# Causal attention with a second, transposed score product in place of probability transposes

## The chip, the cores and the metric

The kernel runs on one core of one Trainium2 chip. Its engines are PE (TensorE, matrix products), DVE (VectorE), ACT (ScalarE), POOL (GpSimd) and SP (SyncE, which here issues DMAs). Times are device microseconds of one execution; the metric is the median over the runs. Each kernel also has one profiled execution, whose instructions and transfers are what the views of the trace show.

## The reference

One layer on 2048 tokens of 1024 features, all in fp32: a layer norm, an attention block with a memory ("infini-attention", 32 heads of 32 features, 4 segments of 512 tokens), a residual, a second layer norm, a mixer block (its own norm, 1024 to 3584 to 1024 with a GELU) and a residual. The attention of a segment s:

```
logits = einsum("bhqd,bhkd->bhqk", qs, ks) * scale + mask      # causal
a_dot  = einsum("bhqk,bhkd->bhqd", softmax(logits), vs)
num    = einsum("bhld,bhde->bhle", phi(qs), M)
den    = einsum("bhld,bhd->bhl", phi(qs), z)[..., None] + 1e-6
o      = g * num / den + (1 - g) * a_dot                       # g = sigmoid(beta) of the head
M      = M + einsum("bhld,bhle->bhde", phi(ks), vs)
z      = z + einsum("bhld->bhd", phi(ks))
```

M (32x32 per head) and z (32 per head) begin at zero, so segment 0 reads nothing from the memory, and what segment 3 would add is never read.

## The kernel before, in words

Products run on PE in a rounded fp32 type. To keep fp32's accuracy each factor is split into a high part (rounded) and a low part (what is left), and a product is three matmuls: high x high, high x low, low x high. A split is a copy on ACT (or DVE) for the high part and a subtraction on DVE (or POOL) for the low one.

The program goes through two halves of 1024 tokens, two segments each. In a half, `attention` loops over 8 groups `g` of four heads and over the half's two segments `sl`. Each such pair is a unit `u`. `dense` computes a unit's projections of keys, queries and values: 3 x 8 x 3 = 72 matmuls of 512 columns, in transposed form (feature by token). Beside them run, by `interleave`, the four heads of the unit before, step by step (`heads`, `slot`). While one unit's projections run, the score products and the softmax of the unit before are done.

Each head is a *slot* of six steps (`PLAN`), and the slots are pipelined over three heads: `cur` has its scores computed, `p1` its probabilities transposed, `p2` multiplied with v. In a slot:

- `qk` (L515): the scores of 128 queries by 128, 256, 384 or 512 keys, as one matmul whose 96 contraction rows hold the three partial products (`stack`, L363, lays them out by DMA from kh, kl, qh, ql). DVE then reduces with the mask (L524): it writes minus the scaled scores to `pr` and their minimum to `mx`; ACT takes the exponential with the row's extreme as bias and sums the row (`soft`, L532).
- `norm` (L534): a reciprocal of the row sums (128x2) on DVE and, on POOL, the multiplication of the probabilities by it and by 1 - g.
- `ptr` (L542): ten 128x128 transposes of the probabilities on PE per head, into PSUM. ACT copies them out as the high part `pth` (L557), `sub` (L560) makes the low part `ptl` on DVE from PSUM and `pth`.
- `av` (L564): eight matmuls into `po`, whose weights are 64 columns wide (v's high and low parts side by side). `av_out` (L582) adds the two halves of `po`, and for the group's last head adds the memory's part on POOL and stores the group.

`late` (L457) handles what is left of a unit beside the next one's projections: transposes of v (L460), the memory read (`pm`, products with queries as weights, so that the result is token by feature; a small reciprocal, L472; a product with it, L474; four transposes back, `pom`, L504) and the memory update (`pmm`, L489, L490). These small matmuls are put one by one between the transposes and PV matmuls (`one_small`).

The order of the instructions on the engines in this stage is that in which the program emits them, subject to the scheduler. After attention, `wo_first` runs the first output products beside the last unit's heads. PSUM has two banks for scores (`qk`), two for transposes (`pt`), one for PV (`av`) and three for projections and small products (`d`).

## Time and profile before

| | us |
|---|---|
| median of 3 runs (2358.27 to 2362.35) | 2360.43 |
| span of the profiled execution | 2354.0 |
| PE busy in that span | 2288.6 |
| DVE busy | 1575.9 |
| ACT busy | 1228.8 |
| POOL busy | 1058.4 |

The profiled execution's span runs from its first to its last instruction and is 6.4 us under the median of the runs. In the page's rows a group of instructions is named by its line, engine and operation, then `out<-in` by the program's names, shapes and count; behind the first bar its busy time in us and the mean duration in ns, behind the second the time for which the engine idled just before these instructions and what ended most of it. In a timeline a row is start (us), duration (us), engine, line, operation, names, shapes and count; an idle time before it stands in brackets with what ended it. Matmul durations include the pipeline's fill, so that consecutive matmuls overlap in these rows.

The attention stage takes about 42 to 520 us and 939 to 1440 us of the span; the rest is the mixer, which the change does not touch.

### The profile page before, as it was taken

To read this page: it belongs to the slowest core of one execution; us is meant where nothing else is said; L and a number is where in the kernel's file an instruction comes from. 1 tells how busy PE (TensorE), PEld (TensorE's weight loads), DVE (VectorE), ACT (ScalarE), POOL (GpSimd) and SP (SyncE) were. 2 spreads that over 40 slices of the span, in tenths; PEclk is the share of its full clock that TensorE was granted. 3 is DMA by queue.
4 is the path that set the end of the run, shared out by engine and by line. 5 is a ranking of instruction groups with operands and counts; after the bars stand their busy time and mean duration, and the time that the engine had idled before them with its cause. 6 is when DMAs were issued, how large, how long until landed. Compare 5 with 4: busy or idle time off the path is not lost.

```text
span 2354.0 us, 35355 instructions
## 1 busy us (share of the span) xinstructions
PE 2288.6 (97%) x11769; PEld 1893.4 (80%) x11769; DVE 1575.9 (67%) x3334; ACT 1228.8 (52%) x2557; POOL 1058.4 (45%) x1037
## 2 busy tenths in 40 slices
PE   7999999999999999999999999999999999999999
PEld 6888888878878887888888877778887888888887
DVE  6777777776655565777777777564566676566753
ACT  5676776785453444777777776363343233222321
POOL 4444444445243442555555545252444564255430
PEclk9999999999999999999999999999999999999999
DMA  5333333345365654433333334466557976576762
GB/s 172 95 89 91 86 81 87 83 115 174 127 196 171 192 161 137 124 83 84 88 83 85 89 93 132 152 198 175 168 176 251 341 254 204 160 251 222 255 219 94
DMA packets 322719, 355.36 MB, mean 151 GB/s; under 512 B 26190, under 2 KB 218730, under 8 KB 322538
## 3 DMA queue, kind: packets, MB, share of 16 engines
q1 hardware_dynamic: 259370, 316.40, 44.7%
q10 hardware_dynamic: 63168, 36.71, 5.2%
q8 instruction: 93, 1.52, 0.3%
q14 instruction: 88, 0.72, 0.1%
HBM read 226.59 MB, written 76.09 MB: 129 GB/s over the span
## 4 chain that ended last, share of the span: by engine, by line
PE 73%; DVE 9%; ACT 7%; DMA 4%; POOL 3%; issue 3%; SPq 1%; ACTq 0%; POOLq 0%; DVEq 0%
PE po L1235 21%; PE bps L856 8%; PE dps L856 5%; PE ppt L555 5%; PE po L575 4%; PE cps L856 4%; PE pqk L523 3%; PE kps L114 2%; PE kps L115 2%; PE kps L116 2%; PE vps L114 2%; PE vps L115 2%; PE vps L116 2%; PE qps L114 2%; PE qps L115 2%
## 5 line engine op out<-in xcount | busy, mean ns | idle before, releaser
L539 POOL TENSOR_SCALAR pr<-pr,nm,gate 128x128 f32<-128x128 f32 (+3 forms) x512 | 320.9, 636 | 400.6 <-DVE nm L536 293.1
L532 ACT ACTIVATE pr<-pr,mx 128x256 f32<-128x256 f32 (+3 forms) x512 | 287.6, 562 | 179.1 <-DVE mx L524 176.5
L524 DVE CUSTOM_DVE_ANT_0 pr<-pqk,mask 128x256 f32<-128x256 f32 (+3 forms) x512 | 243.5, 484 | 37.7 <-PE pqk L523 35.2
L562 DVE TENSOR_TENSOR ptl<-ppt,pth 128x512 fp32r<-128x512 f32 (+1 forms) x384 | 227.2, 597 | 59.5 <-ACT pth L557 57.4
L555 PE MATMUL ppt<-ident,pr 128*128 128x128 f32 x1280 | 223.2, 277 | 1.8 <-DVE ptl L562 1.8
L557 ACT CAST pth<-ppt 128x512 fp32r<-128x512 f32 (+1 forms) x384 | 194.0, 518 | 42.3 <-PE ppt L555 36.7
L1245 DVE TENSOR_TENSOR c<-c,po 128x512 f32<-128x512 f32 x160 | 105.3, 683 | 146.1 <-PE po L1235 146.1
L555 PEld LDWEIGHTS ppt<-ident,pr 128*128 128x128 f32 x1280 | 164.4, 140 | 32.1 <-DVE ptl L562 3.6
L91 POOL TENSOR_TENSOR wl<-wr,wh 128x1024 fp32r<-128x1024 f32 x53 | 126.8, 2392 | 90.8 <-DVE wh L88 31.0
L523 PE MATMUL pqk<-ks,qs 96*128 96x256 f32 (+3 forms) x512 | 163.3, 320 | 1.6 <-DVE mx L524 1.6
L575 PE MATMUL po<-ptl,vs 128*64 128x512 f32 (+3 forms) x512 | 154.8, 312 | 5.9 <-DVE ptl L562 5.7
L575 PE MATMUL po<-pth,vs 128*64 128x512 f32 (+3 forms) x512 | 156.3, 327 | 2.2 <-ACT pth L557 2.1
L1235 PE MATMUL po<-w2h,zh 128*128 128x512 f32 x378 | 120.8, 389 | 0.0
L523 PEld LDWEIGHTS pqk<-ks,qs 96*128 96x128 f32 x512 | 96.6, 189 | 27.1 <-DVE mx L524 7.0
L536 DVE RECIPROCAL nm<-mx 128x2 f32<-128x2 f32 x256 | 42.2, 165 | 109.0 <-ACT pr L532 108.7
L968 POOL TENSOR_TENSOR s<-r 128x512 f32<-128x512 f32 x28 | 43.1, 1540 | 158.9 <-DVE sa L984 117.6
L1105 POOL TENSOR_TENSOR w2r<-w2r 128x512 f32<-128x512 f32 x54 | 85.4, 1593 | 62.3 <-DMA w2r<-in_B_w 62.3
L856 PE MATMUL bps<-zh,sa 128*128 128x512 f32 x336 | 110.7, 390 | 1.6 <-DVE u L998 1.6
L856 PE MATMUL bps<-zh,sb 128*128 128x512 f32 x336 | 111.0, 391 | 0.9 <-DVE u L1010 0.9
L114 PE MATMUL kps<-yh,wh 128*128 128x512 f32 (+1 forms) x264 | 110.2, 417 | 0.6 <-ACT yh L144 0.6
L114 PE MATMUL vps<-yh,wh 128*128 128x512 f32 x256 | 109.0, 426 | 0.2 <-ACT omt L505 0.2
L114 PE MATMUL qps<-yh,wh 128*128 128x512 f32 x256 | 106.8, 417 | 0.0
(237 smaller groups left out, 6748.0 us busy)
## 6 DMA issues: line engine op xcount, KB each, us to landing
hr<-h_dram SPq DMA_DIRECT2D x112, 448.0 KB, 4.8
w2r<-in_B_w SPq DMA_DIRECT2D x122, 256.0 KB, 4.4
r<-in_B_w SPq DMA_DIRECT2D x56, 512.0 KB, 4.6
h_dram<-ht ACTq DMA_DIRECT2D x84, 256.0 KB, 3.8
ks<-kh SPq DMA_DIRECT2D x256, 64.0 KB, 2.0
qs<-qh SPq DMA_DIRECT2D x256, 64.0 KB, 2.0
wr<-in_A_wo SPq DMA_DIRECT2D x32, 512.0 KB, 4.0
wx<-in_B_w SPq DMA_DIRECT2D x56, 256.0 KB, 3.7
```

Of the source, the lines that this page charges most:

```text
L114: nc.tensor.matmul(ps, ah, bh, start=first, stop=False)
L115: nc.tensor.matmul(ps, ah, bl, start=False, stop=False)
L523: nc.tensor.matmul(pqk[:, :n], u["qs"][j][:, i * P:(i + 1) * P], u["ks"][j][:, 0:n], start=True, stop=True)
L524: nc.vector.tensor_tensor_reduce(out=st["pr"][:, offs[i]:offs[i] + n], in0=pqk[:, :n], in1=mask[:, 512 - n:512], op0=ALU.add, op1=ALU.min, ...
L532: nc.scalar.activation(pi, pi, AF.Exp, bias=mx[:, i:i + 1], scale=-1.0, accum_out=mx[:, 4 + i:5 + i])
L539: nc.gpsimd.tensor_scalar(pi, pi, nm[:, 4 + k:5 + k], gate[:, 1, 4 * g + j:4 * g + j + 1], op0=ALU.mult, op1=ALU.mult)
L555: nc.tensor.transpose(ppt[:, o:o + P], pr[:, offs[i] + jk * P:offs[i] + (jk + 1) * P], ident)
L557: nc.scalar.copy(pth[:, base:base + w], ppt[:, :w])
L562: nc.vector.tensor_tensor(o, x0, x1, op=ALU.subtract)
L575: nc.tensor.matmul(po[:, P * jk:], v, st[part][:, koff[jk]:koff[jk] + w], start=(jk, part) == (0, "pth"), stop=(jk, part) == (2, "ptl"))
L856: nc.tensor.matmul(ps, x_[:, c, :], y_[:, c, :], start=first and c == 0 and n == 0, stop=last and c == 3 and n == 2, skip_group_check=True)
L1235: nc.tensor.matmul(ps, x_[:, k], y_[k], start=opens and k == 0 and i == 0, stop=closes and k == self.KP - 1 and i == 2, skip_group_check=True)
```

## The change

Per head, in place of transposed probabilities:

1. The scores are computed as before and reduced with the mask, now only for the row's maximum (`peak`; the reduce writes its elementwise result back into the PSUM tile).
2. The four columns of row extremes (128x4) are transposed on PE (`turn`), copied out in a high part on ACT and a low part on DVE (`row_high`, `row_low`), and sent by two DMAs into rows 96 and 97 of the head's stacked queries `qs`. The stacked keys `ks` have ones in these two rows.
3. The scores are computed a second time, with keys as weights, in transposed form (key by query), over 98 contraction rows: the two added rows subtract the maximum (`scores`).
4. ACT takes the exponential from PSUM into SBUF (`soft`, three per head), POOL zeroes what lies above the diagonal (`cut`), ACT copies the high part (`upper`) and DVE subtracts for the low one (`lower`), both now from the SBUF tile.
5. v's tile is 96 wide: high, low and 32 columns of ones. `po` has 96 rows, of which the last 32 hold the row sums. ACT copies rows 32 to 95 in two instructions (`av_low`). Once per four heads DVE takes the reciprocal of the sums (128x512) and multiplies by it and by 1 - g (`av_out`).

The memory read is turned: the memory is expanded to block-diagonal weights (`blocks`, `mzf`), and numerator and denominator come out feature by token, in 2 x 3 matmuls of 512 columns. ACT adds epsilon, DVE takes a 128x512 reciprocal and multiplies. The memory update becomes 8 matmuls instead of 12, with z kept as one column.

The order of the work is written out: `PLAN` is one list of operations per slot, in which D is one of the 18 projection matmuls that a slot runs beside, m one small matmul of the line, and a digit the head's place in the pipeline (0 cur, 1 the one before, 2 two before). `AT` gives the matmul positions at which the copies, splits and loads of a unit are emitted, `AFTER` those of the small work. PE, DVE, ACT and POOL are held to the order of emission (`in_order(*ATT)`).

```diff
-RA, RH, RS, PD, PS = 1.3, 14, 0.7, 20, 3
-PLAN = ('q1 S2', 'q0 n0 a0', 'q2 t0 a1', 'q3 n2 s0 o', 't1', 's1 t2')
+RA, RH, RS, PD, PS = 1.3, 42, 0.7, 20, 3
+PLAN = ('0q2 0q1 m 2v D D 0x2 m 1t0 1e0 D 1k0 0x1 2o m 1t1 1t3 D 0q3 D 1e1 1t2 1c0 0q0 D D 1k1 1e2 0x3 0x0 '
+        '1s0 D D 0g 1ah0 1k2 D 0h 0l D m 1c1 1al0 1c2 D D D 1s1 m 1s2 D D m m 1ah2 D 1ah3 1ah1 1al1 1al3 '
+        '1al2 D').split()
+AFTER = dict(pkh=3, pkl=3, vh=0, vl=1, den=0, rec=0, mem=0, upd=7)
...
+        def peak(st, i):
+            n = P * (i + 1)
             nc.vector.tensor_tensor_reduce(
-                out=st["pr"][:, offs[i]:offs[i] + n], in0=pqk[:, :n], in1=mask[:, 512 - n:512],
-                op0=ALU.add, op1=ALU.min, scale=-SCALE, scalar=3.0e38, accum_out=st["mx"][:, i:i + 1])
-            soft(st, i)
...
+                out=st["pqk", i][:, :n], in0=st["pqk", i][:, :n], in1=mask[:, 512 - n:512],
+                op0=ALU.add, op1=ALU.min, scale=-1.0, scalar=3.0e38, accum_out=st["mx"][:, i:i + 1])
+        def turn(st):
+            st["pmx"] = psum.tile([P, 512], F32, tag="qk", name="pmx", bufs=2)[0:4, 0:P]
+            nc.tensor.transpose(st["pmx"], st["mx"][:, 0:4], ident)
+        def row_high(st):
+            st["mr"] = ab.tile([4, 2, P], F32R, name="mr", bufs=2)
+            nc.scalar.copy(st["mr"][:, 0, :], st["pmx"])
+        def row_low(st):
+            mr, qs = st["mr"], st["u"]["qs"][st["j"]]
+            nc.vector.tensor_tensor(mr[:, 1, :], st["pmx"], raw(mr[:, 0, :]), op=ALU.subtract)
+            for k in range(2):
+                nc.sync.dma_start(raw(qs[96 + k:97 + k, :]).rearrange("o (i q) -> o i q", i=4), raw(mr[:, k, :]))
+        def scores(st, jk):
...
+            nc.tensor.matmul(st["pst", n][:, o:o + 512 - P * jk], u["ks"][j][:, jk * P:(jk + 1) * P],
+                             u["qs"][j][:, jk * P:512], start=True, stop=True)
+        def soft(st, n):
+            st["p", n] = ab.tile([P, 512], F32, name="pf", bufs=NF)[:, 0:WIDTH[n]]
+            nc.scalar.activation(st["p", n], st["pst", n][:, 0:WIDTH[n]], AF.Exp, scale=SCALE)
+        def upper(st, n):
+            st["h", n] = ab.tile([P, WIDTH[n]], F32R, name=f"pth{n}", bufs=1 + (n == 1))
+            nc.scalar.copy(st["h", n], st["p", n])
+        def lower(st, n):
+            st["l", n] = ab.tile([P, WIDTH[n]], F32R, name=f"ptl{n}", bufs=1 + (n == 1))
+            nc.vector.tensor_tensor(st["l", n], st["p", n], raw(st["h", n]), op=ALU.subtract)
...
+            nc.scalar.copy(u["ot"][b, :], po[32:64, :])
+            nc.scalar.copy(u["den"][b, :], po[64:96, :])
         def av_out(st):
             nc.vector.tensor_tensor(ot[b, :], po[0:32, :], ot[b, :], op=ALU.add)
             if j == 3:
-                if u["omt"] is not None:
+                nc.vector.reciprocal(den, den)
+                nc.vector.scalar_tensor_tensor(ot, ot, gcol[:, 1, g:g + 1], den, op0=ALU.mult, op1=ALU.mult)
+                if u["s"] > 0:
                     nc.gpsimd.tensor_tensor(ot, ot, u["omt"], op=ALU.add)
...
+                def shifted(ps):
+                    read["d"] = tmp("rd")
+                    nc.scalar.activation(read["d"], ps, AF.Identity, bias=eps)
+                def bottom(ps):
+                    then(AFTER["den"], lambda: shifted(ps))
+                    then(AFTER["rec"], lambda: nc.vector.reciprocal(read["d"], read["d"]))
+                def divided(ps):
+                    u["omt"] = ab.tile([P, 512], F32, name="omt", bufs=1)
+                    nc.vector.scalar_tensor_tensor(u["omt"], ps, gcol[:, 0, g:g + 1], read["d"], op0=ALU.mult, op1=ALU.mult)
+                for n, last in ((1, bottom), (0, top_)):
+                    products(("num", "dn")[n], [(lambda ps: ps, x_[:, n], y_)
+                                                for x_, y_ in ((mzh, pqh), (mzh, pql), (mzl, pqh))], last)
```

More of the change, by code (lines that the diff above doesn't have):

```diff
@@ L378, in smalls @@
[L378 to L391 removed]
+                u[name][j] = st
@@ new lines, in dense @@
+            if s > 0:
+                pq = phi(qps, None, position("qe"), position("qr"), position("pq"))
+            at(position("ql"), lambda: low("ql", qps, "qh"))
+            for j in range(4):
+                at(position(f"q{j}"), partial(stacked, "qs", "qh", "ql", (0, 0, 1), (j,)))
+            yield
+            vps = yield from product("v")
+            vt = tmp("vt")
+            at(position("vt"), lambda: nc.scalar.copy(vt, vps))
+            vs = VS[u["n"] % 2]
+            u["omt"] = None
@@ L1279, in pre @@
                     yield
-        interleave(wo_first(half, hts, pre()), rest, RA, RH, RS)
+        with in_order(*END):
+            interleave(wo_first(half, hts, pre()), rest, RA, RH, RS)
+        acts.pop("last")
         if half == 0:
```

503 lines of the change are left out of this document (257 added, 246 removed).

## The prediction

> **What bounds the kernel now.** I read the page first (span, chain), then the busy times of two stretches of the attention stage, then the instructions of TensorE (PE) and VectorE (DVE) in order of time. A *unit* is what the attention loop does for one group of four heads and one segment of 512 tokens: 72 projection products, and beside them the four heads of the unit before. There are 32 units, 16 in each half of the kernel.
>
> ```profile
> span 2354.0 us, 35355 instructions
> PE 73%; DVE 9%; ACT 7%; DMA 4%; POOL 3%; issue 3%; SPq 1%; ACTq 0%; POOLq 0%; DVEq 0%
> ```
> ```profile
> 104.60:168.40 63.80, 62.08 (x379) 52.06 (x378) 48.00 (x147) 44.72 (x115) 30.01 (x38) 1.00 0.33 83
> 1188.70:1251.60 62.90, 62.16 (x378) 52.04 (x377) 48.73 (x149) 45.29 (x116) 33.15 (x41) 1.00 0.33 84
> ```
> ```profile
> 104.62 0.48 PE L114 MATMUL kps<-yh,wh 128*128 128x512 f32 x1
> ...
> 168.41 0.48 PE L114 MATMUL kps<-yh,wh 128*128 128x512 f32 x1
> ...
> 1188.71 0.48 PE L114 MATMUL kps<-yh,wh 128*128 128x512 f32 x1
> ...
> 1251.65 0.48 PE L114 MATMUL kps<-yh,wh 128*128 128x512 f32 x1
> ```
> The columns of the stretches are length, then busy time of PE, weight loads, DVE, ACT and POOL, granted clock, DMA share and GB/s. The four rows after them are the first key product of a unit, so two units (a *pair*) take 63.79 us in the first half and 62.94 us in the second. PE is busy for 62.1 of them at clock 1.00, DVE for 48 to 49 (77%), ACT for 45, POOL for 30 to 33. The attention stage is bound by what PE is given; DVE has some 7 us of slack per unit.
>
> **PE's part of the change.** What a product costs in the stream is the distance from its start to the next start, not its own duration.
>
> ```profile
> 1207.17 0.22 PE L523 MATMUL pqk<-ks,qs 96*128 96x128 f32 x1
> 1207.23 0.39 PE L575 MATMUL po<-pth,vs 128*64 128x512 f32 x1
> 1207.46 0.39 PE L575 MATMUL po<-ptl,vs 128*64 128x512 f32 x1
> 1207.69 0.34 PE L575 MATMUL po<-pth,vs 128*64 128x384 f32 x1
> 1207.87 0.34 PE L575 MATMUL po<-ptl,vs 128*64 128x384 f32 x1
> ...
> 1209.47 0.28 PE L575 MATMUL po<-pth,vs 128*64 128x256 f32 x1
> 1209.59 0.28 PE L575 MATMUL po<-ptl,vs 128*64 128x256 f32 x1
> ...
> 1211.33 0.60 PE L555 MATMUL ppt<-ident,pr 128*128 128x128 f32 x4
> 1211.69 0.48 PE L114 MATMUL vps<-yh,wh 128*128 128x512 f32 x1
> 1212.01 0.40 PE L115 MATMUL vps<-yl,wh 128*128 128x512 f32 x1
> ```
> ```profile
> 1231.71 0.28 PE L555 MATMUL ppt<-ident,pr 128*128 128x128 f32 x1
> 1231.74 0.31 PE L386 MATMUL pm<-mzh,pql 128*128 128x132 f32 x1
> 1231.89 0.51 PE L555 MATMUL ppt<-ident,pr 128*128 128x128 f32 x3
> ```
> So 512 columns cost 0.23 us, 384 cost 0.175, 256 cost 0.12, 128 cost 0.06. Four transposes cost 0.36, and the product behind them 0.32 instead of 0.23. A lone transpose with a narrow product behind it costs 0.18, 0.06 of it the product's; I take 0.14 for a lone one.
>
> The change removes 40 probability transposes per unit (with what they cost the product behind each run) and the memory read's 12 products and 4 transposes. It adds, per head, four score products (96 rows plus the two rows of the maximum) and one transpose of the maxima. The widening of PV from 64 to 96 output rows changes no column count, so I cost it at nothing. New streams per unit:
> - projections 72 x 0.23 = 16.6; scores twice, 2 x 4 x (0.23 + 0.175 + 0.12 + 0.06) = 4.7; PV with its two parts also 4.7: 25.9 us;
> - transposes of maxima and of v, 8 x 0.14 = 1.1: 27.0;
> - segments 0, 1, 2: four key transposes 0.56 and the memory update 4 x 0.12 + 4 x 0.06 = 0.72; segments 1, 2, 3: the memory read 6 x 0.23 = 1.38.
>
> That is 28.3, 29.7, 29.7 and 28.4 us for segments 0 to 3: 58.0 and 58.1 us per pair against 63.8 and 62.9. With 8 pairs in each half: 8 x (5.8 + 4.8) = **85 us less, if PE never waits** (the last unit of a half runs beside the output products, also at PE's rate; I count it alike). About 1 us of waits per pair that the old rows show (62.1 busy of 62.9 to 63.8) I leave in: 16 us given back.
>
> **DVE's part.** The subtractions and the reduce with the mask stay in number. Small reciprocals go; in their place come two reciprocals over a whole 128x512 tile: the row sums out of PV, once per unit, and the memory's denominator in segments 1 to 3. No row shows one that wide; the nearest:
>
> ```profile
> L536 DVE RECIPROCAL nm<-mx 128x2 f32<-128x2 f32 x256 | 42.2, 165 | 109.0 <-ACT pr L532 108.7
> L472 DVE RECIPROCAL rg<-rg 128x8 f32<-128x8 f32 x48 | 9.6, 200 | 1.0
> L70 DVE RECIPROCAL gate<-bb 128x32 f32<-128x32 f32 x1 | 0.3, 299 | 0.0
> L586 DVE TENSOR_TENSOR ot<-po,ot 32x512 f32<-32x512 f32 x128 | 87.0, 680 | 6.6 <-ACT ot L580 3.7
> ```
> From 8 to 32 columns a reciprocal grows by 99 ns, 4.1 ns per column, four times the rate of the 512-wide addition. Carried to 512: 299 + 480 x 4.125 = 2279 ns; I take **2.27 us**. Upper end: the 5.8 ns per column between 2 and 8, 299 + 480 x 5.8 = 3.1 us. Lower end: the 0.68 of the addition. I choose the slope of the widest row, since it is nearest to the size wanted.
>
> The Trainium skill speaks against this change here: "VectorE: DVE Perf Modes", under "First, the fixed hardware budget", has the reciprocal as an iterated divide repeated 8 times, at 0.96 GHz an estimated 8.3 ns per column and 4.3 us for 512. By that each reciprocal is 2 us longer, the fourth rival below. The 299 ns of the 32-column row is hardly above 32 x 8.3 = 267 with nothing for the start, so the trace agrees only if two columns run at once.
>
> What decides is where the first one stands. In the new order of a head's slot the addition that empties PV ("2o"), and for the fourth head the reciprocal and the multiplication behind it, stand on DVE **in front of** the reduces x3 and x0. The transpose of the maxima (g) on PE waits for x0, and the rest of PE's queue waits behind g. DVE's own distances:
>
> ```profile
> 1214.53 0.68 DVE L562 TENSOR_TENSOR ptl<-ppt,pth 128x512 fp32r<-128x512 f32 x1
> 1215.13 0.41 DVE L524 CUSTOM_DVE_ANT_0 pr<-pqk,mask 128x256 f32<-128x256 f32 x1
> 1215.47 0.08 DVE L524 DVE_READ_ACCUMULATOR2_ANT mx<- 128x1 f32 x1
> ...
> 1215.80 0.27 DVE L524 CUSTOM_DVE_ANT_0 pr<-pqk,mask 128x128 f32<-128x128 f32 x1
> 1216.01 0.08 DVE L524 DVE_READ_ACCUMULATOR2_ANT mx<- 128x1 f32 x1
> 1216.73 0.54 DVE L524 CUSTOM_DVE_ANT_0 pr<-pqk,mask 128x384 f32<-128x384 f32 x1
> 1217.19 0.08 DVE L524 DVE_READ_ACCUMULATOR2_ANT mx<- 128x1 f32 x1
> ...
> 1218.28 0.69 DVE L524 CUSTOM_DVE_ANT_0 pr<-pqk,mask 128x512 f32<-128x512 f32 x1
> 1218.90 0.08 DVE L524 DVE_READ_ACCUMULATOR2_ANT mx<- 128x1 f32 x1
> ```
> So x3, x2, x1, x0 take 0.62, 0.46, 0.34, 0.21, a 512-wide subtraction 0.61; I take 0.62 for the addition and 0.65 for the multiplication. From the slot's start, PE reaches g after 10 projection products, four score products, four transposed ones and three small ones: 2.3 + 0.585 + 0.585 + 0.4 = 3.9 us. On DVE, x2 can begin 0.17 after its product, at 0.58, and ends at 1.04, x1 at 1.38, the addition at 2.0. Without a reciprocal x3 waits for its product until 2.7, x0 ends at 3.55, g is on time. With it: 2.0 + 2.27 + 0.65 = 4.92, then the low half of v 5.53, x3 6.15, x0 6.36, **g at 6.5, 2.6 us late**, once per unit.
>
> The second reciprocal is queued in the same slot. In segments 1 and 2 it stands in front of the last subtraction: the denominators end at 7.7, an ACT step at 8.5, the reciprocal at 10.8, the subtraction at 11.15; PE wants the last PV product at 10.46, so 0.8 late, and what queues behind (kl, weight halves, memory product: some 2 us) moves the next slot's x0 by 0.5: 1.3 more. In segment 3 it comes ahead of x2, until 2.35: x1 ends at 3.15, the addition 3.77, reciprocal 6.04, multiplication 6.69, x0 7.5, g 3.7 late in all. Per pair: 2.6 + 3.9 = 6.5 in the first half, 3.9 + 3.7 = 7.6 in the second; 8 x 14.1 = **113 us more**.
>
> **The other engines.** POOL trades four normalizations per head for three masks and drops below its 33 us per pair; ACT gains one copy of PV and loses one exponential: neither is on the path, and each would cost its length in the slot if its 17 us of slack per pair or more were gone. The reduce now writes to PSUM, of which no row tells; its cover is the 0.35 us by which x0 is early, so zero is taken, with up to 0.1 us per slot (13 us) kept. The two rows of the maximum travel by DMA from the subtraction behind g (at 4.6) to the first score product of the next slot (7.4 + 1.25 = 8.65):
>
> ```profile
> ks<-kh SPq DMA_DIRECT2D x256, 64.0 KB, 2.0
> wr<-in_A_wk SPq DMA_DIRECT2D x16, 512.0 KB, 4.4
> ```
> Landing in 2.0 us, it is hidden with 2 us to spare. SP's queue takes 256 more issues among the stacks and the weight loads.
>
> **The sum.** 2354.0 - 85 + 16 + 113 = 2398, with the 6.4 us by which the median (2360.4) stands over the profiled span: 2404.4. By the reciprocal's ends: at 0.68 the first wait falls to 0.9, some 3 us over both kinds of pair: 8 x 3 = 24, so 2354 - 85 + 16 + 24 + 6.4 = 2315; at 3.1 us (0.8 more in 56 places) 2449.
>
> **The rivals.**
> - *Recovery:* the wide reciprocals are cheap, or other DVE work is ready early enough, and PE stays the bound: 2315 (2290 to 2350). For it: PE's sum is firm. Against it: the 299 ns row and a fixed order with g behind. It decides if a reciprocal takes under about 1 us. Chance 0.24.
> - *A draw:* stalls of about 70 us eat the gain, if v's low half or the second reciprocal fall where DVE idles: 8 x 9 = 72 gives 2363 (2350 to 2375). Chance 0.10.
> - *The shared port:* the 12 subtractions per unit used to read PSUM and one SBUF tile; now they read two SBUF tiles, as this instruction does:
>
> ```profile
> 312.37 1.36 DVE L490 SCALAR_TENSOR_TENSOR MZ<-hsel,zc,MZ 128x4 f32<-128x4 f32 x1
> ...
> 340.91 0.22 DVE L490 SCALAR_TENSOR_TENSOR MZ<-hsel,zc,MZ 128x4 f32<-128x4 f32 x1
> ```
> ```profile
> 312.41 1.29 POOL L589 TENSOR_TENSOR ot<-ot,omt 128x512 f32<-128x512 f32 x1 [1.57 <-DVE ot L586]
> ```
> Four columns took 0.22 us, and 1.36 when a POOL addition ran beside them. If a quarter of the 12 waited such 1.14 us, DVE would get 3.4 us per unit more; where a third of that reaches PE, 32 x 1.1 = 36 us: 2440 (2435 to 2500). Chance 0.10. The Trainium skill ("SBUF — State Buffer", "Who interferes with whom") calls the pair of ports an exclusive lock against a DVE instruction with two SBUF inputs; by that rule the sum is this rival's, and these rows agree with it.
> - *Reciprocals twice as long:* at 4.3 us, which no slope of the three rows gives (3.1 at most), 56 times 2.0 us come on top: 2404 + 112 = 2516. Chance 0.03.
> - *The rows come late:* if the small DMAs queue behind a weight load and land in 4.4 us, each slot waits 0.4: 128 x 0.4 = 51, 2455. Chance 0.05.
>
> **The numbers.** The forecast, 2404 with 2375 to 2449 of its own, has 0.48. About 0.2% (4.7 us) is what a measurement of this kernel can tell from no change. Faster: the recovery's 0.24 and 0.02 of the draw, 0.26; same: 0.05; slower: the rest, 0.69. The range 2310 to 2470 leaves out a good part of the recovery below and a few hundredths above.
>
> **What would show it.** Right: one wait per unit on PE at the transpose of the maxima, released by the DVE reduce, 2 to 3 us long; reciprocals of 128x512 near 2.3 us; pairs of 65 to 67 us. Wrong: wide reciprocals under 1 us; PE without a wait at that transpose; pairs near 59 us; or the waits standing at the score products, released by a DMA.

## The result, and the profile after

The changed kernel takes 2575.31 us (median of 4 runs, 2571.96 to 2578.38), 1.091 times the time of the kernel before (95% interval 1.0891 to 1.0922; before 2360.76 beside it). It is slower, as forecast, by 215 us where 44 were forecast; the 2575 lie far above the range.

The page of the kernel after, its span, the busy times and the shares of the chain that ended last; below them, from the groups by line and form in 200 to 500 us, the two wide reciprocals:

```profile
span 2570.2 us, 33619 instructions
PE 2345.7 (91%) x10793; PEld 1885.1 (73%) x10793; DVE 1820.5 (71%) x3049; ACT 1204.6 (47%) x2173; POOL 981.7 (38%) x1005
PE 68%; DVE 15%; issue 6%; ACT 4%; DMA 3%; POOL 3%; SPq 1%; ACTq 0%; DVEq 0%; POOLq 0%
```
```profile
L661 DVE RECIPROCAL den<-den 128x512 f32<-128x512 f32 x8 | 26.8, 3353 | 0.1
L551 DVE RECIPROCAL rd<-rd 128x512 f32<-128x512 f32 x4 | 13.4, 3353 | 3.5 <-ACT rd L547 3.5
```

A reciprocal of 128x512 takes 3.35 us; the forecast had 2.27. DVE's share of the chain goes from 9% to 15%. The next rows are the same view of two pairs of units as in the prediction (length, busy time of PE, weight loads, DVE, ACT, POOL, then granted clock, DMA share, GB/s):

```profile
221.30:296.50 75.20, 64.74 (x321) 51.61 (x320) 61.98 (x131) 43.00 (x91) 23.97 (x34) 0.93 0.27 71
1155.70:1233.20 77.50, 66.34 (x314) 52.61 (x313) 66.00 (x131) 43.80 (x92) 28.89 (x38) 0.91 0.26 69
```

A pair takes 75 to 77 us; the forecast had 65 to 67. Two things stand in these rows: PE idles for 10.5 and 11.2 us of a pair (length less busy time), and it is busy for longer than before (64.7 and 66.3 against 62.1) with fewer instructions, because the granted clock is 0.93 and 0.91. Whom PE waits for, over the whole kernel (us in total, times, longest):

```profile
PE pmx L600 <- DVE mx L594: 65.4, 18, 5.4
PE qps L465 <- DVE vs L533: 53.9, 14, 5.1
PE po L643 <- DVE ptl L636: 38.4, 33, 2.1
PE pqk L590 <- DVE mx L594: 18.6, 14, 2.6
```

The first row is the wait that the prediction named, the transpose of the maxima for the reduces. The second is not in the prediction: the next projection waits for v's low half. How that comes about shows in the order of time on DVE (first fence) and PE (second), around one unit's end:

```profile
230.74 0.68 DVE L659 TENSOR_TENSOR ot<-po,ot 32x512 f32<-32x512 f32 x1
231.43 3.35 DVE L661 RECIPROCAL den<-den 128x512 f32<-128x512 f32 x1
234.82 0.75 DVE L662 SCALAR_TENSOR_TENSOR ot<-ot,gcol,den 128x512 f32<-128x512 f32 x1
235.49 0.68 DVE L533 TENSOR_TENSOR vs<-vn,vs 128x512 fp32r<-128x512 f32 x1
```
```profile
232.24 0.23 PE L590 MATMUL pqk<-ks,qs 96*128 96x128 f32 x1
...
236.22 0.80 PE L465 MATMUL qps<-yh,wh 128*128 128x512 f32 x1 [3.76 <-DVE vs L533]
```

v's transposes lie in one of the three banks for projections and small products (`d`). DVE reads them for the low half, and that subtraction stands behind the reciprocal; until it has read, the next query projection has no bank. In other units a reduce is next in DVE's queue, and then the wait stands at the transpose of the maxima. The clock behind this wait, in stretches of one us (the last column but two is the clock):

```profile
233.00:234.00 1.00, 0.00 (x0) 0.00 (x0) 1.00 (x1) 0.93 (x3) 0.29 (x1) 1.00 0.59 174
234.00:235.00 1.00, 0.00 (x0) 0.00 (x0) 0.96 (x2) 0.00 (x0) 0.00 (x0) 0.70 1.01 298
...
236.00:237.00 1.00, 0.78 (x2) 0.68 (x3) 1.00 (x6) 0.00 (x0) 0.00 (x0) 0.50 0.61 225
...
240.00:241.00 1.00, 1.00 (x4) 0.80 (x3) 0.07 (x2) 0.69 (x1) 0.00 (x0) 0.50 0.04 10
241.00:242.00 1.00, 1.00 (x6) 0.79 (x5) 1.00 (x1) 0.00 (x0) 0.00 (x0) 0.89 0.01 2
242.00:243.00 1.00, 1.00 (x6) 0.79 (x5) 1.00 (x1) 0.00 (x0) 0.00 (x0) 1.00 0.00 0
```

The clock falls inside the wait of 3.8 us, at about 234.4 us, and stays at one half until about 241.2, some 5 us past the end of the wait. So a wait can be paid twice, once as idle time and once as slow products.

### The profile page after: what moved, and what is told of

Same layout as the page of the kernel before. It is cut to its first block, busy times and chain, and to the rows that moved or that the text cites. A ratio compares the mean times of both kernels' runs of the same rounds, so it can differ in the third digit from the quotient of the medians.

```text
span 2570.2 us, 33619 instructions
## 1 busy us (share of the span) xinstructions
PE 2345.7 (91%) x10793; PEld 1885.1 (73%) x10793; DVE 1820.5 (71%) x3049; ACT 1204.6 (47%) x2173; POOL 981.7 (38%) x1005
## 4 chain that ended last, share of the span: by engine, by line
PE 68%; DVE 15%; issue 6%; ACT 4%; DMA 3%; POOL 3%; SPq 1%; ACTq 0%; DVEq 0%; POOLq 0%
PE po L1334 20%; PE bps L955 8%; PE qps L465 6%; PE vps L465 5%; PE dps L955 5%; PE po L643 5%; PE kps L465 5%; DVE den L661 4%; PE cps L955 4%; PE pwo L794 3%; DVE ptl L636 3%; PE pst L618 2%; PE pqk L590 2%; DVE pqk L594 1%; PE pmx L600 1%
## 5 line engine op out<-in xcount | busy, mean ns | idle before, releaser
L627 POOL TENSOR_SCALAR_AFFINE_SELECT pf<-pf 128x128 f32<-128x128 f32 (+1 forms) x384 | 174.8, 458 | 641.9 <-ACT pf L623 528.3
L594 DVE CUSTOM_DVE_ANT_0 pqk<-pqk,mask 128x384 f32<-128x384 f32 (+3 forms) x512 | 245.1, 507 | 99.6 <-PE pqk L590 97.7
L636 DVE TENSOR_TENSOR ptl<-pf,pth 128x512 fp32r<-128x512 f32 (+1 forms) x384 | 291.2, 776 | 24.7 <-ACT pth L632 23.5
L632 ACT CAST pth<-pf 128x512 fp32r<-128x512 f32 (+1 forms) x384 | 200.5, 544 | 22.6 <-POOL pf L627 20.7
L623 ACT ACTIVATE pf<-pst 128x512 f32<-128x512 f32 (+1 forms) x384 | 195.2, 526 | 21.9 <-PE pst L618 18.1
L643 PE MATMUL po<-ptl,vs 128*96 128x512 f32 (+3 forms) x512 | 141.0, 343 | 38.4 <-DVE ptl L636 38.4
L643 PE MATMUL po<-pth,vs 128*96 128x512 f32 (+3 forms) x512 | 161.9, 358 | 3.7 <-ACT pth L632 3.6
L590 PE MATMUL pqk<-ks,qs 96*128 96x384 f32 (+3 forms) x512 | 141.1, 315 | 18.6 <-DVE mx L594 18.6
L618 PE MATMUL pst<-qs,ks 98*128 98x512 f32 (+3 forms) x512 | 148.8, 331 | 3.0 <-ACT pf L623 2.8
L705 POOL TENSOR_TENSOR wl<-wr,wh 128x1024 fp32r<-128x1024 f32 x45 | 119.1, 2646 | 58.1 <-PE qps L465 25.4
L465 PE MATMUL qps<-yl,wh 128*128 128x512 f32 x256 | 118.1, 461 | 0.0
L604 ACT CAST mr<-pmx 4x128 fp32r<-4x128 f32 x128 | 32.4, 253 | 167.1 <-PE pmx L600 166.7
```

The lines of the kernel that those rows point to most:

```text
L465: nc.tensor.matmul(ps, a[:, c, :], b[:, c, :], start=c == 0 and n == 0, stop=c == DC - 1 and n == 2)
L590: nc.tensor.matmul(pqk[:, :n], u["qs"][j][0:96, i * P:(i + 1) * P], u["ks"][j][0:96, 0:n], start=True, stop=True)
L594: nc.vector.tensor_tensor_reduce(out=st["pqk", i][:, :n], in0=st["pqk", i][:, :n], in1=mask[:, 512 - n:512], op0=ALU.add, op1=ALU.min, sca ...
L618: nc.tensor.matmul(st["pst", n][:, o:o + 512 - P * jk], u["ks"][j][:, jk * P:(jk + 1) * P], u["qs"][j][:, jk * P:512], start=True, stop=True)
L623: nc.scalar.activation(st["p", n], st["pst", n][:, 0:WIDTH[n]], AF.Exp, scale=SCALE)
L627: nc.gpsimd.affine_select(p, p, pattern=[[0, 2], [1, P]] if n == 1 else [[1, P]], compare_op=ALU.is_ge, fill=0.0, base=0, channel_multipli ...
```

## The experiments

My theory R: the two wide reciprocals, by their length in DVE's queue, make most of the 215 us, and the waits bring the clock down. Against it: P, the port that DVE shares with POOL; M, the second score products and the transfers of the maxima; C, a clock that falls by itself. Times are medians, ratios are to the kernel before, run beside each.

| kernel | us | ratio (95%) |
|---|---|---|
| after | 2575.3 | 1.0907 (1.0891 to 1.0922) |
| no division at all | 2389.4 | 1.0132 (1.0113 to 1.0151) |
| only the memory's division | 2446.4 | 1.0365 (1.0350 to 1.0381) |
| only the row sums' division | 2527.1 | 1.0711 (1.0695 to 1.0727) |
| half of both divisions | 2477.1 | 1.0497 (1.0478 to 1.0516) |
| v's low half first | 2585.4 | 1.0954 (1.0938 to 1.0971) |
| reciprocal in four pieces | 2594.0 | 1.0998 (1.0980 to 1.1016) |
| exp(-ln x) on ACT, table loads | 2569.8 | 1.0893 (1.0875 to 1.0912) |
| Ln in the copy, one table | 2415.2 | 1.0234 (1.0217 to 1.0250) |
| and pql, mzl on DVE | 2447.1 | 1.0363 (1.0346 to 1.0380) |
| and POOL's weights three steps later | 2412.1 | 1.0217 (1.0199 to 1.0236) |
| and the multiplication on POOL | 2437.5 | 1.0330 (1.0304 to 1.0356) |
| Ln in the copy, DVE's weight copy later | 2396.9 | 1.0160 (1.0141 to 1.0179) |
| and the multiplication later | 2426.9 | 1.0286 (1.0262 to 1.0309) |
| and a sparser last unit | 2425.4 | 1.0275 (1.0244 to 1.0306) |
| no division, PV of 64 rows | 2382.1 | 1.0091 (1.0076 to 1.0106) |

### The reciprocals left out, both and one by one

```diff
-                    then(AFTER["rec"], lambda: nc.vector.reciprocal(read["d"], read["d"]))
...
-                nc.vector.reciprocal(den, den)
```

Both lines out:

> Leaves out the division by the row sums and by the memory's denominator (both 128x512 reciprocals, L661 and L551); everything else of the change stays. Theory R (the two reciprocals hold DVE's queue and so PE, and the waits bring the clock down): the pairs of units go back to 58 to 59.5 us, PE idle under 1.5 us per unit, granted clock 0.98 or more, time 2285 to 2330. Rival P (the shared port and the longer queue of DVE keep PE waiting without them): 2400 to 2460. Rival M (the second score products, their 98 rows and the row transfers are what costs): over 2480, since all of that stays. Rival C (the clock falls by the denser work itself, not by waits): clock stays at 0.93 to 0.96 in the attention stretches, 2380 to 2420.

Only the second out:

> Leaves out the division by the row sums (reciprocal L661, 32 of them) and keeps the memory's (L551, 24 of them). Theory R: most of the loss is L661's, since it is followed at once by v's low half, on which the next projection's bank waits; 2340 to 2410 here. If the two cost alike by the time they take: 24 of 56, so about 2290 + 0.43 x 285 = 2410. Rival M: over 2480.

Only the first out:

> Leaves out the division by the memory's denominator (reciprocal L551, 24) and keeps that by the row sums (L661, 32). Theory R: 2460 to 2530; what this and the kernel with the other one alone save should add up to what leaving out both saves, within 40 us, unless the second wait costs only because the first has used up DVE's slack. Rival M: over 2520.

Without both, 186 of the 215 us are back. Of the kernel without divisions, page and two pairs:

```profile
PE 2290.3 (96%) x10793; PEld 1846.7 (77%) x10793; DVE 1650.9 (69%) x2993; ACT 1202.7 (50%) x2173; POOL 999.5 (42%) x1005
```
```profile
230.30:293.80 63.50, 60.98 (x321) 48.88 (x320) 52.20 (x128) 42.82 (x91) 24.26 (x34) 1.00 0.31 84
1145.60:1208.20 62.60, 61.17 (x313) 48.58 (x313) 52.96 (x126) 43.58 (x92) 29.96 (x38) 1.00 0.32 86
```

The clock is 1.00 again, so rival C falls, though 2389 lies in the range that it gave: it was the waits. As causes of the 186 us M falls as well, since all of the second scores is still there, and P, whose range began at 2400. The same 10793 products take PE 55 us less (2290.3 against 2345.7: half clock), and it idles for 97 us of the span (2387.3 less 2290.3) instead of 224 (2570.2 less 2345.7): 127 us. Together that is the 183 us between the two spans, some 2.3 us of wait and 1.0 us of slow clock for each of the 56 reciprocals (32 units, and 24 with a memory read).

The two kinds add up: 129 us for the 32 of the row sums (4.0 each) and 48 for the 24 of the memory (2.0 each) are 177 of 186. The kernel with the memory's division alone, at 2446, misses the 2340 to 2410 that R gave it; that range was counted from a base of about 2290, and the base is 2389.

But 2389 is outside what R gave this kernel (2285 to 2330): it stands 30 us **above** the kernel before, and its pairs take 63.5 and 62.6 us, hardly less than the old 63.8 and 62.9. A second cause is left, taken up below.

### Half of each reciprocal

```diff
-                nc.vector.reciprocal(den, den)
+                nc.vector.reciprocal(den[:, 0:256], den[:, 0:256])
```
and the same for the memory's.

> Both reciprocals over the first 256 of 512 columns only (leaves out half of both divisions): 1.75 us each by the pieces of 128 (0.94 us) and the whole (3.35 us). None and whole are 186 us apart, 3.3 us for each of 56 reciprocals, just their own time. Theory Q (PE's time goes with DVE's time, one for one): 2389 + 56 x 1.75 = 2487, so 2475 to 2500. Theory K (the half is mostly in DVE's slack and its waits too short for the clock to fall): 2400 to 2455; the clock 0.98 or more.

2477 is theory Q's. With none, half and the whole the time is 2389, 2477 and 2575: the 56 halves (1.75 us each, 98 us) cost 88, the 56 wholes (3.35 us, 188) cost 186. In this kernel's order PE's time goes nearly one for one with DVE's. The waits are shorter (longest 2.7 us, and 40.7 us for the maxima in place of 65.4), but still long enough for the clock, whose mean is 0.977 between 0.993 without and 0.965 with the whole.

### Order and pieces

```diff
-AFTER = dict(pkh=3, pkl=3, vh=0, vl=1, den=0, rec=0, mem=0, upd=7)
+AFTER = dict(pkh=3, pkl=3, vh=0, vl=0, den=0, rec=0, mem=0, upd=7)
```

> Order alone: v's low half is subtracted one small product earlier, ahead of the reciprocal of the row sums in DVE's order; nothing else is changed. Theory Q (what counts is that DVE is away for 4.1 us, whoever is next): the waits of the next projection for v's low half (53.9 us, 14 times) go and come back as waits of the score products or of the transpose of the maxima for the reduces; 2550 to 2580. Rival B (the bank that v's transposes hold is the costly place, and the reduces have room): 14 waits of 3.8 us and the lower clock behind them go, 2470 to 2500.

2585 is nearest to theory Q, 5 us above the 2580 at which its range ends. The waits for v's low half are gone and the first of PE's waits is now

```profile
PE pmx L600 <- DVE mx L594: 132.1, 31, 5.0
```

13 us more than both together before (119.3). The bank of v's transposes, which I had missed, costs nothing by itself.

The pieces, with `2z` for one piece and `2p` for what follows the last:

```diff
-... 0x1 2o m 1t1 1t3 D 0q3 D 1e1 1t2 1c0 0q0 D D 1k1 1e2 0x3 0x0 1s0 D D 0g 1ah0 1k2 D 0h 0l D m ...
+... 0x1 2o 2z m 1t1 1t3 D 0q3 D 2z 1e1 1t2 1c0 0q0 D D 1k1 1e2 0x3 0x0 2z 1s0 D D 0g 1ah0 1k2 D 0h 0l 2z 2p D m ...
...
+                c = slice(k * P, (k + 1) * P)
+                nc.vector.reciprocal(den[:, c], den[:, c])
```

> The reciprocal of the row sums is cut into four pieces of 128 columns, which stand at four places of the same slot: behind the last addition, behind the second query stack, ahead of the first subtraction, and behind the low row of the maxima; the multiplication, the addition of the memory and the store come behind the last. Work and its sum on DVE are the same, if a piece takes a quarter (0.84 us). Theory K (the sum is made of short waits that PE can bear and of a clock that falls only behind long ones): no wait of PE over 2 us in this slot, clock 0.97 or more in the attention loop, 2440 to 2510. Theory Q (DVE's time in that slot is what counts, the slot is full): the same waits in smaller pieces, but the clock still comes back in part; 2500 to 2560. If a piece costs much more than a quarter, the price is fixed and not by columns: over 2575.

Slower than after, and theory K is wrong. The time lies above Q's range too, where I had put pieces that cost much more than a quarter. They cost only somewhat more, 3.77 us in all four, from the groups by line and form in 200 to 500 us:

```profile
L667 DVE RECIPROCAL den<-den 128x128 f32<-128x128 f32 x30 | 28.3, 943 | 0.1
```

Four pieces are thus 0.42 us more per unit, 13 us in all, and the time is 19 longer. The waits did become shorter, but hardly less in sum: the four kinds shown of after come to 172 us here, against 176. Those of PV for the low parts, 38.4 us in after, are now

```profile
PE po L643 <- DVE ptl L636: 106.4, 80, 3.1
```

and the clock stays at 0.961. In this slot, which is full, spreading the work only spread the waits.

### The division off DVE

First as exp(-ln x) on ACT, at the same place:

```diff
-                nc.vector.reciprocal(den, den)
+                nc.scalar.activation(den, den, AF.Ln)
+                nc.scalar.activation(den, den, AF.Exp, scale=-1.0)
```
and the memory's likewise, with Ln in the activation that adds epsilon.

> Both reciprocals become exp(-ln x) on ACT in place, at the same place in the order (row sums: two 128x512 activations between the last addition and the multiplication; memory: Ln in place of the copy with bias, Exp in place of the reciprocal). ACT is at 47% of the span and a 128x512 activation takes 0.60 us in this trace, so the chain gets 1.2 us in place of 3.35. Theory R: near the kernel without any reciprocal, 2290 to 2350, if the functions share one table; if each Ln and the Exp behind it bring a table load (1.28 us each in the trace of after at L873 and L354), 112 loads or 144 us of ACT, part of it before the soft maximum's Exp on the path: 2380 to 2460. Rival M: over 2480.

2570, no gain, and above every expectation but M's, which the kernel without divisions has excluded. Each function brought its load, from the groups of ACT:

```profile
L661 ACT ACT_TABLE_LOAD x8 | 10.3, 1283 | 0.1
L662 ACT ACT_TABLE_LOAD x8 | 10.3, 1283 | 0.1
```
```profile
237.03 0.75 DVE L663 SCALAR_TENSOR_TENSOR ot<-ot,gcol,den 128x512 f32<-128x512 f32 x1 [4.06 <-ACT den L662]
```

DVE is not busy now, but in the fixed order it stands still for 4.06 us at the multiplication, longer than the reciprocal took. I had counted the loads as work of ACT; what counted was the time until DVE could go on.

So the loads had to go. One table set with both functions, loaded once per half, and Ln in the copy of the row sums that is there anyway:

```diff
-            nc.scalar.copy(u["den"][b, :], po[64:96, :])
+            nc.scalar.activation(u["den"][b, :], po[64:96, :], AF.Ln)
...
-                nc.vector.reciprocal(den, den)
+                nc.scalar.activation(den, den, AF.Exp, scale=-1.0)
...
+                    nc.scalar.preload_act_table_set("natural_log_exp_and_others")
```

> Reciprocals on ACT again, as exp(-ln x), but with one table set that holds Ln and Exp loaded once per half (no load in the attention loop), and with Ln taken in the copy of the row sums out of PSUM that is there anyway, so that ACT gets one 128x512 Exp per unit (0.63 us in the trace of the kernel that loads tables) in place of DVE's 3.35 us; the memory's Ln takes the place of the copy with its bias. Theory R (length of DVE's reciprocals; the kernel with exp(-ln x) and loads was slow by its 4.1 us of ACT in the chain, 2.6 of them loads): near the 2389 of the kernel without divisions, 2385 to 2430, clock 0.98 or more. Rival (ACT is late anyway, and any step from DVE to ACT and back costs what the reciprocal cost): 2500 to 2570.

2415: 160 us less than after, with the divisions done, and inside R's range. That is the proof by repair: with the same results computed, the time follows the time for which DVE is held.

### What is left: port, order, last unit, rows of PV

All of these start from the kernel just shown, but for the last, which starts from the one without divisions.

```diff
-                    nc.gpsimd.tensor_tensor(pql, pq["o"], raw(pqh), op=ALU.subtract)
+                    nc.vector.tensor_tensor(pql, pq["o"], raw(pqh), op=ALU.subtract)
```
and the same for `mzl`:

> As the kernel with Ln in the copy, and the low parts of the query features and of the memory (pql, mzl) are subtracted on DVE and not on POOL. Theory P2 (what is left above the kernel before is partly the shared port: the 1.53 us subtraction of 128x256 beside POOL's pql, followed by a PE wait of 1.0 to 1.2 us for ptl in every unit with a memory read): 24 units, so 20 to 30 us under the kernel with Ln in the copy, 2360 to 2400. Rival (the subtraction itself, 0.69 us on DVE, makes as much lateness as the port did): within 8 us of it.

32 us **more**, which neither P2 nor its rival allowed: DVE's own 1.1 us per unit with a memory read (0.68 for `pql`, 0.41 for `mzl`) cost more than the port did. PV's waits for the low parts go from 19.8 to 42.5 us. This kernel also shows when a wait lowers the clock. The first fence is one of its waits and the clock behind it, the second one of the kernel with Ln in the copy:

```profile
81.46 0.36 PE L643 MATMUL po<-ptl,vs 128*96 128x256 f32 x1 [2.01 <-DVE ptl L636]
...
82.00:83.00 1.00, 1.00 (x6) 0.90 (x5) 0.65 (x4) 0.99 (x2) 0.00 (x0) 0.50 1.15 346
83.00:84.00 1.00, 1.00 (x4) 0.81 (x3) 0.97 (x3) 0.61 (x2) 0.00 (x0) 0.50 1.16 352
84.00:85.00 1.00, 1.00 (x4) 0.81 (x3) 0.08 (x1) 0.51 (x2) 0.00 (x0) 0.50 1.06 416
```
```profile
117.25 0.27 PE L600 MATMUL pmx<-ident,mx 128*4 128x128 f32 x1 [1.40 <-DVE mx L594]
...
118.00:119.00 1.00, 1.00 (x6) 0.85 (x5) 1.00 (x3) 0.64 (x2) 0.22 (x2) 1.00 0.83 285
```

The 1.40 us leave it at 1.00, the 2.01 us halve it, but the length of the wait alone does not decide. The kernel with `pql` and `mzl` on DVE has this wait seven times in its first half, 1.96 to 2.01 us long, and the clock falls behind four of them only. All stretches of half clock in this trace begin on one grid of 3.41 us. The next rows are two neighbouring stretches of that grid around the wait shown, and two around the wait of 2.00 us that ends at 418.13:

```profile
78.57:81.98 3.41, 1.40 (x10) 1.05 (x9) 3.41 (x5) 0.13 (x1) 1.41 (x1) 1.00 0.52 143
81.98:85.40 3.42, 3.42 (x11) 2.84 (x10) 1.72 (x6) 2.54 (x5) 0.24 (x1) 0.50 1.07 357
...
416.49:419.90 3.41, 1.77 (x9) 1.55 (x10) 3.15 (x9) 1.34 (x3) 0.17 (x1) 1.00 0.89 256
419.90:423.32 3.42, 2.35 (x12) 1.91 (x11) 2.69 (x7) 3.42 (x8) 0.89 (x3) 1.00 0.27 88
```

The first wait lies within one stretch, where PE idles for 2.01 us, and the next stretch runs at 0.50. The second is cut by the edge at 416.49: PE idles for 1.64 us of the stretch behind it, and the clock stays at 1.00.

POOL's low part of the queries' weights, three steps later:

```diff
-AT = dict(... hq=120, oq=124, ...)
+AT = dict(... hq=120, oq=127, ...)
```

> As the kernel with Ln in the copy, and the low part of the queries' weights is subtracted three steps later on POOL (oq 124 to 127), so that its 2.7 us no longer lie beside DVE's last two subtractions of a slot (3.20 us together beside it, 1.03 without). Theory P3 (there the shared port does cost, since PE waits 1.02 to 1.15 us for ptl in 15 units): 15 to 20 us under the 2415 of that kernel, 2393 to 2402. Rival (the weights' subtraction only meets another copy of DVE, or the next slot's selection, which wait instead): within 5 us of 2415.

2412, no difference that can be told, and nothing tested: the edit changed POOL's order but not the moment, since POOL was idle and waited for something else (126.79 us against 126.55). To move it, what it waits for had to move, the copy of the high part on DVE:

```diff
-AT = dict(... hq=120, oq=124, ...)
+AT = dict(... hq=124, oq=127, ...)
```

> As the kernel with Ln in the copy; DVE's copy of the queries' weights (hq 120 to 124) stands behind the last two subtractions of its slot, not ahead of them, so that POOL's 2.7 us for the low part, which waits for that copy, cannot start beside them. (Three steps later on POOL alone had changed the order but not the moment: it started at 126.79 us and not at 126.55, and the waits for ptl stayed at 1.15 us.) Theory P3 (the shared port there makes the 1.02 to 1.15 us waits for ptl in 15 units): these waits go, 15 to 18 us less, 2395 to 2402. Rival (the copy comes 0.7 us into the next slot's reduces and waits appear there): 2408 to 2420.

2397, 18 us less, as P3 had it. Two fences of DVE and POOL in order of time, first with Ln in the copy alone, then with the copy moved:

```profile
126.33 3.19 DVE L636 TENSOR_TENSOR ptl<-pf,pth 128x512 fp32r<-128x512 f32 x2
126.55 2.69 POOL L705 TENSOR_TENSOR wl<-wr,wh 128x1024 fp32r<-128x1024 f32 x1 [1.82 <-PE qps L465]
```
```profile
125.81 1.03 DVE L636 TENSOR_TENSOR ptl<-pf,pth 128x512 fp32r<-128x512 f32 x2 [0.24 <-ACT pth L632]
...
127.58 2.41 POOL L705 TENSOR_TENSOR wl<-wr,wh 128x1024 fp32r<-128x1024 f32 x1 [2.33 <-PE pmm L419]
```

The same two subtractions take 1.03 us alone and 3.19 beside POOL's. The port is a cost, of some 18 us. The edit also takes the copy, 0.6 us of DVE, from ahead of the subtractions, but of the 2.7 us by which they end earlier 2.2 are their shorter duration.

The multiplication on POOL (with the later weights of the test before the last, which had made no difference), and the multiplication later on DVE (with the copy moved). In the first the factor 1 - g goes into the Exp on ACT, as a bias:

```diff
-                nc.vector.scalar_tensor_tensor(ot, ot, gcol[:, 1, g:g + 1], den, op0=ALU.mult, op1=ALU.mult)
+                nc.gpsimd.tensor_tensor(ot, ot, den, op=ALU.mult)
```

> As the kernel with the moved subtraction of weights, and the multiplication by the inverse row sums goes from DVE to POOL; the gate is folded into the Exp as a bias (its logarithm, made once). DVE then no longer waits for the Exp of the row sums (0.63 us) and loses 0.75 us of work per unit. Theory Q (DVE's time in the slot behind a unit's last head sets PE's wait): the waits for v's low half and for the reduces of 1.07 and 1.40 us per unit go, 32 units by about 1.2 us, 2355 to 2375. Rival (POOL's two passes of 128x512 lie on the shared port beside the subtractions of the same slot): 2390 to 2420.

```diff
-... 0h 0l D m 1c1 ...
+... 0h 0l 2p D m 1c1 ...
```

> As the one with the weights' copy moved, and the multiplication by the inverse row sums with what follows it stands behind the low row of the maxima, some 3 us later in the same slot; the Exp on ACT stays. DVE then does not wait for the Exp. Theory Q2 (1.4 us of DVE ahead of v's low half and the reduces make the waits of 1.07 and 1.40 us): these go to 0.3 us or less, 20 to 27 us less than the kernel before it, 2370 to 2382. Rival (the slot is full: the 0.75 us only come ahead of the subtractions, and PE waits for ptl in place): within 6 us of the kernel before it.

Both are slower, by 25 and 30 us than the kernels they start from, and above what either theory gave them. In both the waits that I wanted to remove are gone (none for v's low half or the transpose of the maxima among the largest). In their place stand, in the first, waits of 1.0 to 1.3 us for the low parts, of 1.1 us for the high parts and of 2.3 us for the activation that takes the memory's denominator out of its bank:

```profile
PE po L645 <- ACT pth L634: 29.6, 21, 4.0
PE po L645 <- DVE ptl L638: 28.7, 24, 2.1
PE num L421 <- ACT rd L549: 19.7, 14, 2.3
```

and in the second

```profile
PE po L643 <- DVE ptl L636: 22.7, 17, 2.2
PE pqk L590 <- DVE mx L594: 18.2, 13, 2.7
```

where the kernel before it had waits of 1.1 and 1.4 us: less often, but about 1.9 us long, and every second unit of the first half takes 32.4 to 36.0 us in place of 31.1. The slot is full, and two waits of at most 1.4 us cost less than one of 1.9, behind which the clock falls in most of these units.

```diff
-RA, RH, RS, PD, PS = 1.3, 42, 0.7, 20, 3
+RA, RH, RS, PD, PS = 0.9, 60, 0.7, 20, 3
```

> As the one with the late multiplication, and the last unit's heads are taken less densely beside the output products (0.9 places per product up to the 60th, 0.7 behind, in place of 1.3 up to the 42nd). In the kernel without divisions the output products of the two halves take 126.5 and 122.0 us against 116 and 117.8 before, with 13.9 and 11.7 us of waits (for pth, ptl, the reduces) in the last unit. Theory E (the new slot is a longer chain per head than the old one and too short beside few products): 8 to 20 us less. Rival (the waits are only moved to the end, where heads without products are left): within 5 us, or longer.

1.5 us less than the kernel it starts from, within its spread: the rival. That does not mean that the last unit costs nothing. The same 20 us in the kernel before (first row) and in the one without divisions (second), beside the first output products:

```profile
525.00:545.00 20.00, 18.31 (x110) 14.69 (x111) 15.78 (x49) 14.72 (x35) 9.71 (x11) 1.00 0.56 184
```
```profile
525.00:545.00 20.00, 14.27 (x59) 10.46 (x57) 10.95 (x23) 11.92 (x24) 7.36 (x9) 0.83 0.27 74
```

PE idles for 5.7 us of the second, 4.6 of them in two waits for the high part of the probabilities, and the clock is 0.83. I put this down to the longer chain of a head (scores, maxima, DMA, scores, exponential, mask, copy, subtraction) beside a last unit, where PE has less to do; no run shows it. The ratio of the interleave did not mend it.

```diff
-            nc.tensor.matmul(st["po"][:, P * jk:], u["vs"][:, 4 * jk + j, :], st[part, n][:, o:o + 512 - P * jk],
+            nc.tensor.matmul(st["po"][:, P * jk:], u["vs"][:, 4 * jk + j, 0:64], st[part, n][:, o:o + 512 - P * jk],
```

Here `po` has 64 rows too, and the copy of the sums reads rows 32 to 63 in place of 64 to 95.

> As the kernel without both divisions, and PV has 64 output rows as before the change (no ones; leaves out the row sums). My sum took the widening from 64 to 96 rows at nothing. Theory N (nothing): 2384 to 2394, the same as 2389. Rival W (a weight load of 96 columns in place of 64 shows behind the narrow products, 64 loads per pair): 10 to 40 us less, 2350 to 2380.

2382 against 2389, between the two expectations. The intervals of the ratios (1.0076 to 1.0106 and 1.0113 to 1.0151) do not meet, so the wider PV is worth some 7 us where my sum had nothing. It is small.

No kernel here beats the one before. The best that computes everything is the one with Ln in the copy and the weights' copy moved, 2396.9; taking 18 us off the kernel without divisions gives about 2371 (an estimate from these two runs), so even free divisions and no collision with the weights would end 10 us above.

## Why the direction was right and the size wrong

**The reciprocal was mis-sized: +60 us.** "I take 2.27 us" was an extrapolation from 32 columns to 512 by the slope between 8 and 32. It takes 3.35. Between 128 columns (943 ns) and 512 (3353) the slope is 6.28 ns per column, and 943 less 128 of these leaves 139 ns to start: the rows of 2 and 8 columns (165 and 200 ns) fit that line to within 14 ns, the row of 32 is 41 ns under it. I chose the slope of the one row that was a single instruction (x1) over that of the rows with 256 and 48, and called the other slope, 5.8, the upper end. 56 times 1.08 us are 60. The estimate that I had worked out from the Trainium skill's "VectorE: DVE Perf Modes" (under "First, the fixed hardware budget"), 8.3 ns per column and 4.3 us, is about as far off to the other side.

**The place was right in part, and it did not matter.** I put 2.6 us of lateness per unit on the transpose of the maxima and let the low half of v pass as 0.6 us in DVE's queue. In 14 of the 32 units the wait stands at the next projection instead, for the bank that v's transposes hold. The order experiment shows that the place hardly changes the time (10 us more without the waits for v). At 2.27 us the rule that the runs give, one for one, would have been 127 us where my arithmetic of slots gave 113.

**The clock was not in the sum.** I had costed waits as waits. About 1.0 of the 3.3 us that a reciprocal costs is PE at half clock behind the wait. That my 113 us lie near the 127 is luck: I counted 0.89 us of lateness for each us of a reciprocal and nothing for the clock, and the runs show 0.68 of wait and 0.30 of slow clock.

**PE's 85 us did not come.** This is the second large error: pairs without divisions were to take 59.0 us with the old waits and take 63.5 and 62.6, which is 8 x (4.5 + 3.5) = 64 us. By busy time, 8 x (3.0 + 3.1) = 49 of these are PE's streams: 61.0 and 61.2 us where I had 58.0 and 58.1. The other 15 are waits. The sum was absolute, each product priced at the distance inside a run of like ones, with nothing for the changes from one kind to the next, and compared with a measured pair that has these changes in it. Added up from start to start in the second of these pairs, without idle time, the projections take 35.0 us where the sum had 33.1, PV 11.2 for 9.4, both score products 10.4 for 9.4, and only the small transposes less, 0.8 for 2.8. The projections of the old pair took 34.9 already, so their 1.9 us were never a gain. A difference of like with like would have warned: 40 transposes of 128 columns go, 5120 columns per unit; four heads times 1280 columns of second scores come, 5120 columns. PE is given no less to stream. Measured in the same way the transposes took 6.0 us of the old pair, and the second score products take 5.4 of the new one. Over the whole kernel its busy time is 2290.3 us without divisions, and 2288.6 before.

The other 34 us of the 98 lie outside the pairs. In the stretch of the first output products of the first half (505 to 655 us) PE's waits come to 15 us, against 5 before (500 to 640 us); with the slow clock there, and the like in the second half, I take this to be the better part of it. The rest I did not trace, and its cause stays open.

**The rivals.** The shared port was real, but smaller than its 36 us: 18, and at POOL's low part of the weights. What it costs beside `pql` and `mzl` is not shown, only that it is less than their subtraction on DVE. The rows of the maxima did not come late: no DMA stands among the 20 largest of PE's waits. The recovery asked for reciprocals under 1 us. "Reciprocals twice as long" (2516, chance 0.03) was nearest in time, with a price between its 4.3 and my 2.27.

**The balance.** The forecast was 171 us low: 60 for the length of the reciprocals, 13 for what one of them costs beyond that (186 measured against 113 + 60), and 98 by which the kernel without divisions missed the sum for it: 49 of PE's streams, 15 of waits in the pairs, 34 outside the pairs.

## What to carry to other kernels

Where the engines are held to a written order and the second busiest has little slack inside each slot, price a new instruction by its full length on the path, before any arithmetic about who waits. Extrapolate a duration from the rows with many instructions, and check the line on the third row. When work is exchanged on the bounding engine, compare columns with columns and instructions with instructions first; a sum of ideal prices set against a measured stretch shows a gain even where nothing is taken away.

## What the runs showed of the hardware

- PE's clock: in each of these traces it is 1.00 or 0.50, and the stretches at 0.50 begin on one grid of 3.41 us and last one to four of its steps (less where the trace ends). Taking the 17 traces together, from 45 us on, a step at 1.00 in which PE idled for more than 1.9 us was always followed by 0.50 (283 steps), and one with less than 1.38 us never; between the two it went either way. So a wait of 2.0 us halved the clock where it lay within one step and did not where the edge of a step cut it. The Trainium skill, "TensorE: Matmul & The Clock Gate", Part 1, has the low state come after at least one idle window of about 3.4 us; here windows with work in them were enough, as the one with 1.40 us of PE's work shows.
- A reciprocal of float32 took 0.94 us for 128 columns on DVE, 1.75 for 256 and 3.35 for 512, which is 0.14 us and 6.28 ns per column.
- Ln and Exp, each called after the other, brought 110 table loads of 1.283 us for 112 calls, and none in the loop when a set with both had been loaded once ahead of it.
- Two subtractions of SBUF tiles on DVE took 1.03 us alone and 3.19 beside a subtraction on POOL, which itself took 2.41 and 2.69. This agrees with the exclusive lock for which the prediction names the Trainium skill.
